# Value product of a top-k attention: the last 64 rows of both heads as one block diagonal matrix that opens the accumulation

## The chip, the cores and the metric

One NeuronCore of one Trainium2 chip. The metric is device time in microseconds (us) of one execution. PE (TensorE) has two queues in the profile: PE for matrix products and PEld for weight loads. DVE is VectorE, ACT is ScalarE, POOL is GpSimd, and SP issues nearly all input transfers. Each engine works through its own instructions in the order in which the program was written, and waits at the first one whose operands are not there.

## The reference

Attention over 2 batches, 8 heads, 576 positions and 64 columns a head, in float32. Of each row of scores only the 32 largest are kept. Its output feeds a first mixture of four experts and a second layer of three products under a maximum.

```python
scores = scale * q @ k.T                                   # 576 x 576 for a batch and head
kth = np.partition(scores, -32, axis=-1)[..., -32:-31]
attn = softmax(np.where(scores >= kth, scores, -1e9))
x = (attn @ v) as [1152, 512]                              # heads side by side
out = sum_e p[:, e:e+1] * (relu(x @ w1[e]) @ w2[e])        # p: domain_probs over their row sum
return max(out @ m1, out @ m2, out @ m3) @ mo
```

## The kernel before

**Pairs.** The attention works on two heads at once, the head pair `hp` (four of them), and on a tile of 128 rows of the 1152 (nine). That gives 36 pairs, in the order chunk `c` (tiles 0 and 1, 2 and 3, 4 and 5, 6 to 8), head pair, tile. A `Pair` goes through: scores on PE (L350), copies of them to SBUF on ACT (L358), four rounds of the eight largest on DVE (L371, L373), the exponential on ACT (L384), and the mask that keeps the 32 largest (`mask`). The mask is one DVE instruction with the row sum (L391), except in the first eight pairs, where `ON_POOL` puts it on POOL as two instructions a head (L394, L395) and the sum on ACT (L399). Then the probabilities are transposed on PE (L409, L414) and copied to SBUF by ACT as `pt[0]`, `pt[1]` (L412) and `pt[2]` (L417). The row sums go through `guard` (ACT, L422), `recip` (DVE, L428), `spread` (ACT, L432) and a transposition (PE, L437), and `norm` (DVE, L462) multiplies the value product by them.

**The value product** (`pv`, L452 and L455). 576 positions are four blocks of 128 and a rest of 64. `pt[0]` and `pt[1]` hold the four blocks of either head; `pt[2]` holds the rest of head 0 in partitions 0 to 63 and that of head 1 in 64 to 127. The tile `vt` of a batch and head pair holds the values in the same way: 4 blocks of 64 columns a head, and a ninth block with the rest of head 0 above that of head 1. Head 0 goes to output partitions 0 to 63, head 1 to 64 to 127. So there are eight products of 128 rows by 64 columns, and after them two of 64 by 64. The tile in the middle (`MIXED`, tile 4) belongs to both batches and is done in two parts of 64 columns each; so 36 pairs make 40 parts.

**Slots.** `attention` writes the order of all engines by slots, eight to a pair: a function is put at a slot, and the slots are then issued one after the other. Pair n begins at slot 8n. `split_k` and `split_q` (ACT L261 and L293, then POOL L262 and L294) and the loads `load_k` and `load_q` (SP, L247) stand some slots before the first pair that needs them. `kraw` and `qraw` have one buffer each, so that a load waits until POOL has split the one before. `load_v` (SP, L266) stands at the slot where the first pair of a batch and head pair begins: pairs 0, 2, 4 and 6 for batch 0, and pairs 16, 18, 20 and 22 for batch 1. The tile `vt` has five buffers. `load_gates` stands at slot 20: a transfer issued by SP (L121), and four small DVE instructions (L123 to L127) that wait for it.

**Products beside it.** From about the eighth pair on, the experts' products (PE, L589 to L591) are woven in between by a count of DVE and PE time. Their weights come through SP (L175) into three buffers, ACT rounds them (`whi`, L224), and POOL (L230, or DVE for some of the late ones) computes the remainder `wlo`. After the last pair only such products are left.

Of the kernel before, what the change touches and what calls it, by code (L numbers as in the profile page):

```python
# [10 lines left out]
F32 = mybir.dt.float32  # L11
# [37 lines left out]
def kernel(  # L49
# [14 lines left out]
    nc = tc.nc  # L64
    B, HP, D, _, S = k.shape
    NT, DM = out.shape
    E = gates.shape[2]
    P = 128
# [3 lines left out]
    NR = S // P  # L72
# [15 lines left out]
    kv = ctx.enter_context(tc.tile_pool(name="kv", bufs=2))  # L88
# [22 lines left out]
    def pe(n):  # L111
        clock["pe"] += n / 2400.0

    def bank(name):
        return pg.tile([P, 512], F32, tag="g", name=name)
# [126 lines left out]
    kraw, kT, vt, qraw, qT = {}, {}, {}, {}, {}  # L242
# [19 lines left out]
            sub(out=d[D:, j], in0=t[D:, j], in1=d[D:, j].bitcast(F32), op=ALU.subtract)  # L262

    def load_v(b, hp):
        t = vt[b, hp] = kv.tile([P, 2 * NR + 1, D], F32, tag="v", bufs=5, name="vt")
        nc.sync.dma_start(out=t, in_=v[b, hp])  # L266

    def load_q(c, hp, heads=slice(0, 2)):
        slots = SLOTS[c]
# [61 lines left out]
    class Pair:  # L331
# [109 lines left out]
        def pv(self):  # L441
            assert {("pt", i) for i in range(3)} <= self.did
            ps = bank("psv")
            pe((NR + 1) * 512)
            if self.t == MIXED:
                parts = [(0, slice(0, TAIL)), (1, slice(TAIL, P))]
            else:
                parts = [(0 if self.t < MIXED else 1, slice(0, P))]
            for b, cols in parts:
                for r in range(NR):  # L450
                    for j in range(2):
                        nc.tensor.matmul(ps[j * D:(j + 1) * D, cols], lhsT=vt[b, self.hp][:, j * NR + r, :],  # L452
                                         rhs=self.pt[j][:, r, cols], start=r == 0, stop=False)
                for j in range(2):
                    nc.tensor.matmul(ps[j * D:(j + 1) * D, cols], lhsT=vt[b, self.hp][j * D:(j + 1) * D, 2 * NR, :],  # L455
                                     rhs=self.pt[2][j * D:(j + 1) * D, cols], start=False, stop=True)
            self.x = ps

        def norm(self):
# [17 lines left out]
    def attention():  # L477
# [18 lines left out]
        for key, n in first_use.items():  # L496
            s0 = 8 * n
            if n == 0:
                if key[0] == "k":
                    at_slot(-60, load_first)  # L500
                    at_slot(-50, split_first)
                    free["k"] = free["q"] = -50
                    at_slot(s0, load_v, *key[1:])
                continue
            load, split = (load_k, split_k) if key[0] == "k" else (load_q, split_q)
            at = max(s0 + options(n)["scores"] - (SPLIT_K if key[0] == "k" else SPLIT_Q), free[key[0]] + 2)
            at_slot(max(at - 15, free[key[0]] + 1), load, *key[1:])
            at_slot(at, split, *key[1:])
            free[key[0]] = at
            if key[0] == "k":  # L510
                at_slot(s0, load_v, *key[1:])
# [129 lines left out]
    def experts(n, c):  # L641
        tiles = CHUNKS[c]
        N = len(tiles) * P
        if c < len(CHUNKS) - 1:
            acc = [xp.tile([P, DM], F32, tag="acc", bufs=sum(len(x) for x in CHUNKS[:-1]), name="acc") for _ in tiles]
        else:

            acc = [kv.tile([P, (2 * NR + 1) * D], F32, tag="v", bufs=5, name="acc")[:, 0:DM] for _ in tiles]
        accs.update(zip(tiles, acc))

        def half1(i, u):
# [262 lines left out]
```

## Time and profile before

| | us |
|---|---|
| Median of three runs | 791.98 |
| Lowest and highest run | 791.22, 792.48 |
| Profiled execution, first to last instruction (its own time) | 793.7 |
| PE busy in it | 737.3 (93%) |
| DVE busy | 659.2 (83%) |
| POOL busy | 533.4 (67%) |
| ACT busy | 480.5 (61%) |

The profiled execution was 1.7 us longer than the median. The attention ends at about 484 us of it; all pairs lie before that and the rest is products. Busy shares are means over stages that differ: in the first 100 us PE is far from full and DVE is not, and after 600 us it is the other way round. A busy PE is not a PE at its peak, since the ends of matrix products are modelled; how fast it works is seen from the starts of its instructions.

### The profile page before, as it was taken

How to read it: one execution, taken by the hardware profiler on the slowest of the kernel's cores; microseconds unless marked ns; L12 is line 12 of the kernel's file. 1: busy time of each engine (PE TensorE's matmuls, PEld its weight loads, DVE VectorE, ACT ScalarE, POOL GpSimd, SP SyncE). 2: the span in 40 equal slices, each digit the busy share in tenths (PEclk: the TensorE clock that was granted, in tenths of full speed). 3: DMA queues.
4: the chain of work that ended last, by engine and by line, in shares of the span. 5: the costliest groups of instructions: out<-in, count | busy, mean ns of one | idle time of the engine just before them, and what ended most of it. 6: DMA issues, size and time to landing. Idle time of an engine off the chain costs nothing.

```text
span 793.7 us, 13648 instructions
## 1 busy us (share of the span) xinstructions
PE 737.3 (93%) x4726; PEld 656.9 (83%) x4726; DVE 659.2 (83%) x1247; ACT 480.5 (61%) x1021; POOL 533.4 (67%) x438
## 2 busy tenths in 40 slices
PE   3776799979999999999999999989999899999998
PEld 2554699879888888988898897978999699899996
DVE  6999989978999999999999996989999783243241
ACT  5666758666776777767777665655565352443441
POOL 2787968859888979688888696667564553253330
PEclk9976699989999999999999999999999999999999
DMA  3430145445466445353644455867878554262421
GB/s 99 119 108 3 52 146 160 139 134 181 116 177 202 126 139 171 116 159 114 168 132 133 134 164 167 293 221 244 263 235 256 168 190 136 93 212 65 169 100 40
DMA packets 48485, 119.92 MB, mean 151 GB/s; under 512 B 7712, under 2 KB 17952, under 8 KB 48416
## 3 DMA queue, kind: packets, MB, share of 16 engines
q1 hardware_dynamic: 40208, 110.40, 45.1%
q10 hardware_dynamic: 8208, 8.65, 3.1%
q8 instruction: 37, 0.61, 0.3%
q14 instruction: 32, 0.26, 0.1%
HBM read 110.38 MB, written 8.65 MB: 150 GB/s over the span
## 4 chain that ended last, share of the span: by engine, by line
PE 43%; DVE 32%; DMA 8%; POOL 6%; issue 5%; ACT 3%; SPq 2%; ACTq 0%; POOLq 0%; DVEq 0%
DVE m L371 12%; PE ps L589 12%; PE ps L591 11%; PE ps L590 11%; DVE work L373 11%; DVE p L391 5%; POOL wlo L230 5%; DMA raw<-in_w_dram 3%; SPq L247 2%; PE pso L591 2%; PE pso L589 2%; PE pso L590 2%; DMA raw<-in_m_dram 2%; DMA kraw<-in_k_dram 2%; ACT whi L224 1%
## 5 line engine op out<-in xcount | busy, mean ns | idle before, releaser
L230 POOL TENSOR_TENSOR wlo<-raw,whi 128x512 fp32r<-128x512 f32 x260 | 354.6, 1391 | 155.7 <-ACT whi L224 154.9
L224 ACT ACTIVATE whi<-raw 128x1024 fp32r<-128x1024 f32 x164 | 170.6, 1058 | 66.9 <-PE ps L591 30.8
L589 PE MATMUL ps<-xl,whi 128*128 128x256 f32 (+1 forms) x512 | 155.0, 303 | 0.8 <-DVE h L669 0.8
L371 DVE MAX8 m<-work 128x8 f32<-128x576 f32 x216 | 154.5, 742 | 0.1
L591 PE MATMUL ps<-xh,wlo 128*128 128x256 f32 (+1 forms) x512 | 152.5, 298 | 0.0
L590 PE MATMUL ps<-xh,whi 128*128 128x256 f32 (+1 forms) x512 | 152.5, 298 | 0.0
L373 DVE MATCH_REPLACE8 work<-m,work 128x576 f32<-128x576 f32 x144 | 106.3, 739 | 0.0
L230 DVE TENSOR_TENSOR wlo<-raw,whi 128x1024 fp32r<-128x1024 f32 x34 | 49.6, 1460 | 66.2 <-ACT whi L224 54.9
L589 PEld LDWEIGHTS ps<-xl,whi 128*128 128x128 f32 x512 | 98.6, 193 | 1.9 <-DVE h L669 1.0
L590 PEld LDWEIGHTS ps<-xh,whi 128*128 128x128 f32 x512 | 98.6, 193 | 0.9
L591 PEld LDWEIGHTS ps<-xh,wlo 128*128 128x128 f32 x512 | 98.6, 193 | 0.0
L589 PE MATMUL ps<-wlo,h 128*128 128x512 f32 x192 | 78.1, 407 | 0.0
L590 PE MATMUL ps<-whi,h 128*128 128x512 f32 x192 | 75.7, 394 | 0.0
L591 PE MATMUL ps<-whi,h 128*128 128x512 f32 x192 | 75.7, 394 | 0.0
L591 PE MATMUL ps<-x2h,wlo 128*128 128x384 f32 x216 | 72.8, 337 | 0.0
L589 PE MATMUL ps<-x2l,whi 128*128 128x384 f32 x216 | 72.8, 337 | 0.0
L590 PE MATMUL ps<-x2h,whi 128*128 128x384 f32 x216 | 72.6, 336 | 0.0
L409 PE MATMUL psp<-ident,p 128*128 128x128 f32 x288 | 49.5, 300 | 24.9 <-POOL p L395 16.4
L391 DVE SCALAR_TENSOR_TENSOR p<-s,m,p 128x576 f32<-128x576 f32 x57 | 72.0, 1263 | 0.0
L350 PE MATMUL pss<-kT,ql 128*128 128x288 f32 x160 | 54.5, 355 | 14.0 <-DVE ql L294 7.5
L207 POOL TENSOR_TENSOR narrow<-narrow,raw 128x256 int32<-128x256 int32 x48 | 38.7, 806 | 42.0 <-DVE narrow L204 11.7
L409 PEld LDWEIGHTS psp<-ident,p 128*128 128x128 f32 x288 | 37.3, 153 | 30.9 <-POOL p L395 19.7
(96 smaller groups left out, 1639.7 us busy)
## 6 DMA issues: line engine op xcount, KB each, us to landing
raw<-in_w_dram SPq DMA_DIRECT2D x128, 512.0 KB, 3.8
raw<-narrow SPq DMA_DIRECT2D x36, 512.0 KB, 3.3
raw<-in_m_dram SPq DMA_DIRECT2D x36, 256.0 KB, 4.6
narrow<-narrow ACTq DMA_DIRECT2D x48, 128.0 KB, 3.8
kraw<-in_k_dram SPq DMA_DIRECT2D x14, 288.0 KB, 4.4
raw<-in_mo_dram SPq DMA_DIRECT2D x12, 256.0 KB, 4.1
vt<-in_v_dram SPq DMA_DIRECT2D x8, 288.0 KB, 4.4
out_dram<-ob ACTq DMA_DIRECT2D x9, 256.0 KB, 2.0
```

The source lines that it names most:

```text
L207: nc.gpsimd.tensor_tensor(out=out.bitcast(I32), in0=out.bitcast(I32), in1=last, op=ALU.add)
L224: nc.scalar.activation(out=hi, in_=raw, func=AF.Copy)
L230: on.tensor_tensor(out=lo[:, x], in0=raw[:, x], in1=hi[:, x].bitcast(F32), op=ALU.subtract)
L247: nc.sync.dma_start(out=out[half * D:(half + 1) * D], in_=src)
L350: nc.tensor.matmul(ps[:, 0:SH], lhsT=l, rhs=r, start=i == 0, stop=i == len(mm) - 1)
L371: nc.vector.max(m[:, 8 * r:8 * r + 8], src)
L373: nc.vector.match_replace(out=self.w[j], in_to_replace=m[:, 8 * r:8 * r + 8], in_values=src, imm_value=NEG)
L391: nc.vector.scalar_tensor_tensor(out=p, in0=s, scalar=kth, in1=p, op0=ALU.is_ge, op1=ALU.mult, accum_out=total)
L409: nc.tensor.transpose(ps[:, r * P:(r + 1) * P], self.p[:, part, part * TAIL + r * P:part * TAIL + (r + 1) * P], ident)
L589: nc.tensor.matmul(ps, lhsT=lh, rhs=rl, start=first, stop=False)
L590: nc.tensor.matmul(ps, lhsT=lh, rhs=rh, start=False, stop=False)
L591: nc.tensor.matmul(ps, lhsT=ll, rhs=rh, start=False, stop=last)
```

## The change

`vt` gets a tenth block of 64 columns. The ninth keeps the rest of head 0 in partitions 0 to 63 and gets zeros in 64 to 127; the tenth gets zeros in 0 to 63 and the rest of head 1 in 64 to 127. Blocks nine and ten side by side are then a block diagonal matrix of 128 by 128. The transfer is the same as before and fills blocks one to nine; three POOL instructions behind it, in `load_v`, clear the upper half of block ten, copy the lower half of block nine into it, and clear that lower half. In `pv` one product of 128 by 128 with `pt[2]` opens the accumulation for both heads, and the eight products of 128 by 64 follow, of which the last ones close it.

```diff
     def load_v(b, hp):
-        t = vt[b, hp] = kv.tile([P, 2 * NR + 1, D], F32, tag="v", bufs=5, name="vt")
-        nc.sync.dma_start(out=t, in_=v[b, hp])
+        t = vt[b, hp] = kv.tile([P, 2 * NR + 2, D], F32, tag="v", bufs=5, name="vt")
+        nc.sync.dma_start(out=t[:, 0:2 * NR + 1], in_=v[b, hp])
+        nc.gpsimd.memset(t[0:D, 2 * NR + 1], 0.0)
+        nc.gpsimd.tensor_copy(out=t[D:, 2 * NR + 1], in_=t[D:, 2 * NR])
+        nc.gpsimd.memset(t[D:, 2 * NR], 0.0)
...
             for b, cols in parts:
+                both = vt[b, self.hp][:, 2 * NR:2 * NR + 2, :].rearrange("p a d -> p (a d)")
+                nc.tensor.matmul(ps[:, cols], lhsT=both, rhs=self.pt[2][:, cols], start=True, stop=False)
                 for r in range(NR):
                     for j in range(2):
                         nc.tensor.matmul(ps[j * D:(j + 1) * D, cols], lhsT=vt[b, self.hp][:, j * NR + r, :],
-                                         rhs=self.pt[j][:, r, cols], start=r == 0, stop=False)
-                for j in range(2):
-                    nc.tensor.matmul(ps[j * D:(j + 1) * D, cols], lhsT=vt[b, self.hp][j * D:(j + 1) * D, 2 * NR, :],
-                                     rhs=self.pt[2][j * D:(j + 1) * D, cols], start=False, stop=True)
+                                         rhs=self.pt[j][:, r, cols], start=False, stop=r == NR - 1)
```

A tile that shares the buffers of `vt` in the last chunk of the experts is made as wide as the new `vt`. Line numbers behind L269 are three higher in the changed kernel until `pv`. The orders of DVE, ACT and SP stay the same; POOL gets 24 instructions, PE loses one product in each of 40 parts.

On POOL, around the first `load_v` (slot 0), before. `ql` and `kT` are the splits of queries and keys, `s` and `p` the mask of pair 0; what a row waits for stands in brackets:

```order
L294 TENSOR_TENSOR ql<-qraw,qh 128x2x256 [waits DMAHW1_49,DMAHW0_49,Activation_49]
L262 TENSOR_TENSOR kT<-kraw,kT 64x576 [waits DMAHW3_49,Activation_49,Pool_49]
L262 TENSOR_TENSOR kT<-kraw,kT 64x576 [waits Activation_49]
L394 TENSOR_SCALAR s<-s,m_188 128x576 [waits DVE_49,Activation_49,Pool_49]
L395 TENSOR_TENSOR p<-p,s 128x576 [waits Pool_49]
L394 TENSOR_SCALAR s<-s,m_196 128x576 [waits DVE_49,Activation_49]
L395 TENSOR_TENSOR p<-p,s 128x576 [waits Pool_49]
L294 TENSOR_TENSOR ql<-qraw,qh 128x2x256 [waits DMAHW4_49,DMAHW5_49,PE_49,Activation_49]
L262 TENSOR_TENSOR kT<-kraw,kT 64x576 [waits DMAHW7_49,Activation_49,Pool_49]
```

The same place on POOL in the changed kernel:

```order
L262 TENSOR_TENSOR kT<-kraw,kT 64x576 [waits Activation_49]
L267 MEMSET vt 64x64
L268 COPY vt<-vt 64x64 [waits DMAHW0_49]
L269 MEMSET vt 64x64 [waits Pool_49]
L397 TENSOR_SCALAR s<-s,m_188 128x576 [waits DVE_49,Activation_49,Pool_49]
L398 TENSOR_TENSOR p<-p,s 128x576 [waits Pool_49]
L397 TENSOR_SCALAR s<-s,m_199 128x576 [waits DVE_49,Activation_49]
L398 TENSOR_TENSOR p<-p,s 128x576 [waits Pool_49]
L297 TENSOR_TENSOR ql<-qraw,qh 128x2x256 [waits DMAHW4_49,DMAHW5_49,PE_49,Activation_49]
L262 TENSOR_TENSOR kT<-kraw,kT 64x576 [waits DMAHW7_49,Activation_49,Pool_49]
```

The three new instructions stand between the key split and the mask of pair 0, and the copy waits for the transfer of `vt`; the mask and the next splits stand behind it.

On PE, at the first value product, before (`pss` are scores, `psv` the value product):

```order
L350 MATMUL pss<-kT,qh 128x288
L350 MATMUL pss<-kT,ql 128x288 [waits Activation_49]
L350 MATMUL pss<-kT,qh 128x288
L452 MATMUL psv<-pt,vt 64x128 [waits DMAHW0_49,Activation_49]
L452 MATMUL psv<-pt,vt 64x128 [waits Activation_49]
L452 MATMUL psv<-pt,vt 64x128 x6
L455 MATMUL psv<-pt_295,vt 64x128 [waits Activation_49]
```

And in the changed kernel:

```order
L353 MATMUL pss<-kT,qh 128x288
L353 MATMUL pss<-kT,ql 128x288 [waits Activation_49]
L353 MATMUL pss<-kT,qh 128x288
L455 MATMUL psv<-pt_298,vt 128x128 [waits DMAHW0_49,Activation_49]
L458 MATMUL psv<-pt,vt 64x128 x8
```

The product with the rest (`pt_295`, now `pt_298`) has moved from the end of the part to its head, and with it the wait for the last copy of ACT.

## Rows read from the trace of the kernel before

**Rows 1.** Page: shares of the chain that ended last, engines, then lines.

```profile
PE 43%; DVE 32%; DMA 8%; POOL 6%; issue 5%; ACT 3%; SPq 2%; ACTq 0%; POOLq 0%; DVEq 0%
```

**Rows 2.** Windows: stretch; busy us (instructions) of PE, PEld, DVE, ACT, POOL; clock, DMA.

```profile
60.00:100.00 40.00, 27.54 (x159) 21.73 (x158) 39.97 (x90) 28.18 (x79) 34.41 (x27) 0.67 0.11 31
100.00:130.00 30.00, 30.00 (x237) 27.44 (x237) 27.29 (x57) 20.87 (x45) 23.62 (x20) 1.00 0.53 162
130.00:180.00 50.00, 45.90 (x333) 40.53 (x332) 45.72 (x93) 32.42 (x71) 36.49 (x32) 0.93 0.43 134
180.00:230.00 50.00, 49.73 (x346) 43.49 (x345) 47.03 (x98) 34.76 (x78) 45.05 (x39) 1.00 0.54 160
```

**Rows 3.** Waits of DVE from 200 to 480 us: total, times, longest.

```profile
DVE acc L698 <- PE ps L591: 0.6, 1, 0.6
```

**Rows 4.** Chain of waits in order of time, start and us, up to 60 us.

```profile
28.08 1.42 POOL kT L262
...
31.31 4.30 DMA gate<-in_gates_dram
```

**Rows 5.** Timeline of DVE: start, us, instruction, idle before it and what ended that.

```profile
29.22 0.15 DVE L428 RECIPROCAL rr<-rs 128x2 f32<-128x2 f32 x1
...
35.63 0.19 DVE L123 TENSOR_REDUCE gs<-gate 128x9 f32<-128x36 f32 x1 [1.45 <-DMA gate<-in_gates_dram]
...
41.46 0.15 DVE L428 RECIPROCAL rr<-rs 128x2 f32<-128x2 f32 x1
```

**Rows 6.** Timeline of POOL around the first load of values.

```profile
16.12 2.77 POOL L262 TENSOR_TENSOR kT<-kraw,kT 64x576 fp32r<-64x576 f32 x2 [1.19 <-ACT kT L261]
18.99 1.73 POOL L394 TENSOR_SCALAR s<-s,m 128x576 f32<-128x576 f32 x1
```

**Rows 7.** Tile view of `vt`, its first transfer: issue, and issue to landing.

```profile
L266 SPq DMA_DIRECT2D vt<-in_v_dram x1: 585/585/585, 20.1 to 20.1; - x1
...
DMA to landing us min/median/max: 4.5/4.5/4.5
```

**Rows 8.** POOL's groups by shape: count, busy us, mean ns of one.

```profile
L475 POOL TENSOR_TENSOR xl<-xt,xh 128x128 fp32r<-128x128 f32 x36 | 20.5, 571 | 3.5 <-ACT xh L474 3.4
L278 POOL MEMSET qraw<- 128x128 f32 x8 | 1.4, 201 | 0.1
```

**Rows 9.** Timeline of PE around a value product at full clock.

```profile
126.11 0.60 PE L409 MATMUL psp<-ident,p 128*128 128x128 f32 x4
126.55 0.27 PE L414 MATMUL psp<-ident,p 128*128 128x128 f32 x1
...
130.92 1.09 PE L452 MATMUL psv<-pt,vt 128*64 128x128 f32 x16
131.94 0.43 PE L455 MATMUL psv<-pt,vt 64*64 64x128 f32 x4
132.31 0.33 PE L437 MATMUL psr<-ident,rb 128*128 128x128 f32 x1
```

**Rows 10.** Timeline of SP: the fifth and the last issue of `vt`.

```profile
209.09 1.45 SPq L266 DMA_DIRECT2D vt<-in_v_dram  x1
...
287.09 0.33 SPq L266 DMA_DIRECT2D vt<-in_v_dram  x1
```

**Rows 11.** Tile view of `vt`: all eight transfers, issue to landing.

```profile
DMA to landing us min/median/max: 3.1/4.4/5.0
```

**Rows 12.** Timeline of POOL behind these two loads, and its next idle times.

```profile
211.17 1.85 POOL L294 TENSOR_TENSOR ql<-qraw,qh 128x768 fp32r<-128x768 f32 x1
...
223.84 1.30 POOL L662 TENSOR_TENSOR h<-raw,h 128x512 fp32r<-128x512 f32 x1 [1.34 <-ACT h L661]
...
289.73 1.86 POOL L294 TENSOR_TENSOR ql<-qraw,qh 128x768 fp32r<-128x768 f32 x1
294.96 5.57 POOL L230 TENSOR_TENSOR wlo<-raw,whi 128x512 fp32r<-128x512 f32 x4 [3.38 <-ACT whi L224]
```

**Rows 13.** Timeline of ACT: a weight that waits for its transfer.

```profile
225.87 1.06 ACT L224 ACTIVATE whi<-raw 128x1024 fp32r<-128x1024 f32 x1 [1.16 <-DMA raw<-in_w_dram]
```

More of the change, by code (lines that the diff above doesn't have):

```diff
@@ L646, in experts @@
         else:
-            acc = [kv.tile([P, (2 * NR + 1) * D], F32, tag="v", bufs=5, name="acc")[:, 0:DM] for _ in tiles]
+            acc = [kv.tile([P, (2 * NR + 2) * D], F32, tag="v", bufs=5, name="acc")[:, 0:DM] for _ in tiles]
         accs.update(zip(tiles, acc))
```

## The prediction

> **What bounds the kernel now.** I read the shares of the chain of waits first: PE 43%, DVE 32% [rows 1]. So two engines take turns, and the question for each part of the change is whose turn it falls into. The windows and DVE's waits answer that. From 60 to 100 us DVE is busy 39.97 of 40 us and PE 27.54 [rows 2]: DVE is the bound. From 100 to 230 us DVE has holes, 2.71 + 4.28 + 2.97 = 9.96 us of 130 [rows 2]: there PE, POOL and the weights lead. From 200 to 480 us DVE waits once, for 0.6 us [rows 3]: it is the bound again, although PE looks nearly full. Behind about 484 us there are only products. All value products lie before that, mostly where DVE leads. A shorter PE can give back little there, while anything that stops DVE is paid in full.
>
> Then I read the start of the chain in order of time. It runs from a key split on POOL, 28.08 us [rows 4], through SP (the next key load had to wait for that split, and the loads of `vt` and of the gates stand behind it) to the transfer of the gates, issued at 31.31 us and landing 4.30 us later [rows 4]. DVE has idled 1.45 us for it when it goes on at 35.63 us [rows 5]. So here POOL's own order already sets DVE's time, and this is where the change puts three instructions.
>
> **PE: one product for two.** At full clock the 16 records of L452 start at 130.92 us, the four of L455 at 131.94, the next instruction at 132.31 [rows 9]. L455 so costs 132.31 - 131.94 = 0.37 us a part; that goes. The new opening product is two records of 128 by 128. Nearest are the four transposes of that size, 0.44 us from the first to the next instruction [rows 9], 0.11 each, so 0.22 us for two. From below: two records at the pace of L452, 1.02 / 16 each, 0.13 us; from above: no cheaper than what it replaces, 0.37 us. I take 0.22, since the transposes have the same shape, and a gain of 0.15 us a part (0 to 0.24). Of the 40 parts 7 lie before 94 us, where DVE leads; 33 remain, 33 x 0.15 = 5.0 us of PE time. What of it reaches the end is bounded by DVE: from 200 us on at most the 0.6 us that DVE waits [rows 3], and before that half a dozen parts, 6 x 0.15 = 0.9 us, in front of a stage that waits for weights as well. I take 0.5 us, and 0 to 2.1 for the range (11 parts at 0.19). The wait for the last copy of ACT comes first instead of last. It can cost a few tenths of a us where PE now waits for ACT before `pv`; those places are mostly in DVE's stretches, and I count nothing.
>
> The four records of L455 take 0.092 us each, those of L452 0.064 [rows 9]: the small ones are no cheaper. The Trainium skill, TensorEngine Tiling (Array Packing), Key Properties, speaks against this half of the change: tiles of the array work in parallel, so two products of 64 by 64 on different rows and columns need no more time than the one that replaces them; it also says that a change of the tiling mode drains the array, and one such change goes. By the first rule alone the gain on PE would be 0 and the sum 0.5 us higher; by both it is the drain, and the 0.15 us agree with that.
>
> **POOL: the first load, the dear one.** POOL finishes two key splits at 16.12 + 2.77 = 18.89 us and begins the mask of pair 0 at 18.99 [rows 6]. In the changed order the two clearings and the copy stand between, and the copy waits for `vt`. SP issues that transfer only at 20.1 us, because it too stands behind a load that waits for these splits, and it lands 4.5 us later [rows 7], at 24.6. So POOL, which works in order, stands still from about 19.1 to 24.6 us. The copy itself isn't in the trace of before; nearest are a clearing of 128 by 128, 0.20 us, and a two-operand instruction of that size, 0.57 us [rows 8]. With half the columns I take 0.25 us for the copy, 0.15 for a clearing and 0.1 for starts: the mask starts at 24.6 + 0.5 = 25.1 instead of 18.99, **6.1 us late** (5.9 to 6.6). Nothing covers it: behind it on POOL are the mask (four instructions without a gap), the query split and the key splits of rows 4, which all move by 6.1. With the key split SP's queue moves, with that the gate transfer, from 31.31 to 37.4 us, and DVE goes on at 37.4 + 4.3 = 41.7 instead of 35.63 us. DVE will already have waited on the way, at the `recip` of 29.22 us [rows 5], since the row sums of pair 0 come after its mask; that wait lies inside the same 6.1 us. From there to 94 us DVE has no holes into which the loss could go, so the whole program moves by 6.1 us.
>
> **The second load.** SP issues its transfer just ahead of the gates, so at about 30.7 + 6.1 = 36.8 us, and by the median of 4.4 us [rows 11] it lands at 41.2. POOL comes there at about 39: the splits end at 28.08 + 1.42 + 6.1 = 35.6 us [rows 4], and the mask of one head follows, 1.73 us [rows 6] and a second instruction nearly as long. It waits 2.2 us and works 0.5. The next `recip`, at 41.46 us [rows 5], moves to 47.6 by itself; the mask of the other head now ends at about 45, and ACT's work between the two fills most of what is left. I count 0, and up to 1.0 for the range. Loads three and four have landed when POOL comes to them: 0.5 us of work each, in POOL's idle time (34.41 of 40 us busy [rows 2]).
>
> **Loads five to eight.** They lie where DVE leads. The fifth is issued at 209.09 us [rows 10], lands 4.4 us later by the median [rows 11], and POOL comes there at 211.17 [rows 12]: it waits 2.3 us. The last: 287.09 + 4.4 - 289.73 = 1.8 us. Four of these at a mean of 2.05, with 0.5 us of work each, are 10.2 us of POOL. POOL's own idle times come next: 1.34 us before 223.84, 3.38 us before 294.96 [rows 12]. So most is caught up before anyone waits. What may get through is a weight: SP's weight loads wait for POOL to free a buffer, and ACT at 225.87 us already waits 1.16 us for one [rows 13], with the next exponential behind it. Of the fifth load's 2.8 us 1.34 are caught up by then; half of the other 1.5 is my price, 0.7 us, from 0 up to half of the 10.2.
>
> **The sum.** 6.1 - 0.5 + 0 + 0.7 = +6.3 us. The profiled span would go from 793.7 to 800.0 us; against the median of the runs, 791.98, that is **798.3 us**, since nothing in the sum depends on the 1.7 us between them.
>
> **The rivals.** (a) The later waits aren't caught up: every us in which POOL stands still at loads five to eight reaches DVE or PE. Then 791.98 + 6.1 - 0.5 + 10.2 = 807.8 us; for it speaks that SP, ACT and POOL hang on each other by three weight buffers, against it POOL's idle times and DVE's single wait of 0.6 us in the whole stretch. (b) The first loss is taken back between 100 and 230 us, where DVE has 9.96 us of holes: 792 us, no change. It needs a stage that is led by weights which are not delayed themselves. Against: their first loads stand on SP behind a load that waits for POOL, and their remainders on POOL behind the masks, so they are late too. (c) Faster: POOL's wait falls into slack that I don't see and PE leads everywhere; then 33 parts at 0.15 give 791.98 - 5.0 = 787.0 us. It decides from the point at which the gate transfer is not what DVE waits for; the 1.45 us of idle with that name speak against it, and so does DVE's full stretch from 200 on. (d) The opening product costs more than it saves; that is a tenth of a us a part in DVE's shadow, within the range of the forecast.
>
> **Chances.** Forecast 0.72, (a) 0.14, (b) 0.08, (c) 0.06. Slower by over 0.2% (above 793.6 us; about what a measurement of this kernel can tell from no change) is forecast and (a), 0.86; within it (b), 0.08; faster (c), 0.06. The range: below, 791.98 + 5.9 - 2.1 and another us for a shifted clock, which runs in steps before 110 us (0.67 of full from 60 to 100 [rows 2]), 794.8; above, 791.98 + 6.6 + 5.1, rounded up for the second load's part, 804.0, half way into (a).
>
> **What would show it.** Right: in the new trace POOL's first mask begins near 25 us with an idle time that ends by the transfer of `vt`; DVE idles about 5 us at its first `recip` and some 3 at the gates; the gates' work starts near 41.7 us; the start of L452 to the instruction behind the part is shorter by about 0.37 us, with some 0.22 in front; and the last pair ends about 6 us later. Wrong: POOL starts its mask at 19 us (the copy did not wait), or DVE's idle time between 100 and 230 us falls by as much as it gained before, or weight loads after 209 us leave DVE holes of 2 us each.

## The result, and the profile after

The changed kernel takes 798.33 us (median of 8 runs, 795.84 to 802.14), the kernel before 792.2 (8 runs, 790.15 to 794.82): 6.1 us more, as forecast. The ratio of the two is 1.0089, with a 95% interval of 1.0065 to 1.0112, so 5 to 9 us. The profiled execution spans 796.4 us; here every run's time is 1.8 us above its span, so that the profiled execution of before, with a span of 793.7, took 795.5 us and was longer than any of these eight. Differences of time are therefore taken from the medians below, and the profiles are used for where time goes. Single executions of one kernel differ by up to 10.6 us (23 runs of before, further down, lie between 785.13 and 795.77), and their granted clocks don't order them (the correlation of time and clock is -0.09 to -0.17 in the three sets of before).

The page of after, part 4: the chain of waits by engine and by line. It answers to [rows 1].

```profile
DVE 38%; PE 37%; DMA 8%; POOL 8%; issue 4%; ACT 3%; SPq 2%; ACTq 0%; POOLq 0%; DVEq 0%
DVE m L374 14%; DVE work L376 13%; PE ps L592 10%; PE ps L594 10%; PE ps L593 10%; DVE p L394 5%; DMA raw<-in_w_dram 4%; POOL wlo L230 3%; DVE h L672 2%; DMA vt<-in_v_dram 2%; PE pso L594 2%; PE pso L592 2%; PE pso L593 2%; SPq L247 2%; POOL kT L262 1%
```

The transfer of `vt`, which nobody had waited for in before, is now on the chain with 2%. DVE's share has grown from 32 to 38%, PE's has fallen from 43 to 37%.

The timeline of POOL at the first two loads (start, us, instruction; in brackets idle time and what ended it), the place of [rows 6]:

```profile
15.88 2.78 POOL L262 TENSOR_TENSOR kT<-kraw,kT 64x576 fp32r<-64x576 f32 x2 [1.75 <-ACT kT L261]
18.72 0.14 POOL L267 MEMSET vt<- 64x64 f32 x1
24.32 0.24 POOL L268 COPY vt<-vt 64x64 f32<-64x64 f32 x1 [5.46 <-DMA vt<-in_v_dram]
24.62 0.15 POOL L269 MEMSET vt<- 64x64 f32 x1
24.86 1.73 POOL L397 TENSOR_SCALAR s<-s,m 128x576 f32<-128x576 f32 x1
...
41.27 0.24 POOL L268 COPY vt<-vt 64x64 f32<-64x64 f32 x1 [2.51 <-DMA vt<-in_v_dram]
```

POOL stands still for 5.46 us and begins the mask of pair 0 at 24.86 us, where it had begun at 18.99. Behind it the chain can be followed step by step. This is the chain of waits of after in order of time (start, us, what):

```profile
18.72 0.16 POOL vt L267
...
19.87 4.40 DMA vt<-in_v_dram
...
24.86 1.73 POOL s L397
...
29.87 1.42 POOL p L398
...
32.59 2.79 POOL kT L262 x2
35.40 0.48 SPq L247
...
37.20 4.14 DMA gate<-in_gates_dram
...
41.36 0.20 DVE gs L123
```

Mask, key split, the key load on SP, the gates, DVE: the chain of [rows 4], with POOL's wait in front. The gates were issued at 31.31 us and are now at 37.20. DVE shows both places at which it stood; its timeline, beside [rows 5]:

```profile
33.30 0.17 DVE L431 RECIPROCAL rr<-rs 128x2 f32<-128x2 f32 x1 [4.12 <-ACT rs L425]
...
41.36 0.19 DVE L123 TENSOR_REDUCE gs<-gate 128x9 f32<-128x36 f32 x1 [3.08 <-DMA gate<-in_gates_dram]
...
47.56 0.14 DVE L431 RECIPROCAL rr<-rs 128x2 f32<-128x2 f32 x1
```

The last row is the `recip` that stood at 41.46 us: 6.10 us late, and so are the instructions that follow it up to 92 us. The four later loads that POOL waits for are in the list of its waits from 200 to 300 us (who waited for what: us in total, times, longest):

```profile
POOL vt L268 <- DMA vt<-in_v_dram: 6.6, 4, 2.1
```

And PE, beside [rows 9], timeline at full clock:

```profile
122.46 0.40 PE L594 MATMUL ps<-whi,h 128*128 128x512 f32 x1
122.69 0.38 PE L455 MATMUL psv<-pt,vt 128*128 128x128 f32 x2
123.01 1.09 PE L458 MATMUL psv<-pt,vt 128*64 128x128 f32 x16
124.03 0.33 PE L440 MATMUL psr<-ident,rb 128*128 128x128 f32 x1
```

From the last product ahead to the instruction behind the part are 124.03 - 122.46 = 1.57 us. Before they were 132.31 - 130.60 = 1.71 (the product ahead of the part in [rows 9] started at 130.60). So a part became 0.14 us shorter.

### The profile page after: what moved, and what is told of

Read it like the earlier page. It is cut to its first block, busy times and chain, and to the rows that moved or that the text cites. A ratio compares the mean times of both kernels' runs of the same rounds, so it can differ in the third digit from the quotient of the medians.

```text
span 796.4 us, 13528 instructions
## 1 busy us (share of the span) xinstructions
PE 733.0 (92%) x4646; PEld 662.8 (83%) x4646; DVE 657.2 (83%) x1247; ACT 482.0 (61%) x1021; POOL 537.7 (68%) x462
## 4 chain that ended last, share of the span: by engine, by line
DVE 38%; PE 37%; DMA 8%; POOL 8%; issue 4%; ACT 3%; SPq 2%; ACTq 0%; POOLq 0%; DVEq 0%
DVE m L374 14%; DVE work L376 13%; PE ps L592 10%; PE ps L594 10%; PE ps L593 10%; DVE p L394 5%; DMA raw<-in_w_dram 4%; POOL wlo L230 3%; DVE h L672 2%; DMA vt<-in_v_dram 2%; PE pso L594 2%; PE pso L592 2%; PE pso L593 2%; SPq L247 2%; POOL kT L262 1%
## 5 line engine op out<-in xcount | busy, mean ns | idle before, releaser
L394 DVE SCALAR_TENSOR_TENSOR p<-s,m,p 128x576 f32<-128x576 f32 x57 | 68.5, 1202 | 0.0
```

What stands on the lines that cost most here:

```text
L394: nc.vector.scalar_tensor_tensor(out=p, in0=s, scalar=kth, in1=p, op0=ALU.is_ge, op1=ALU.mult, accum_out=total)
```

## The experiments

Theory: POOL, in its order, waits for the first transfer of `vt`, and what stands behind it on POOL makes DVE late. Rival 1: the new product, or its earlier wait for ACT's last copy, is the loss. Rival 2: the waits at loads five to eight are. The first four kernels ran on one chip, beside 29 runs of the kernel before (792.45 us).

**The three POOL instructions moved ten slots behind the load.** PE's part is that of the change. `late_v` says for which loads they move, here for all eight.

```diff
         nc.sync.dma_start(out=t[:, 0:2 * NR + 1], in_=v[b, hp])
+        if not late_v(b, hp):
+            fill_v(b, hp)
+
+    def late_v(b, hp):
+        return True
+
+    def fill_v(b, hp):
+        t = vt[b, hp]
         nc.gpsimd.memset(t[0:D, 2 * NR + 1], 0.0)
         nc.gpsimd.tensor_copy(out=t[D:, 2 * NR + 1], in_=t[D:, 2 * NR])
...
                 at_slot(s0, load_v, *key[1:])
+                if late_v(*key[1:]):
+                    at_slot(s0 + 10, fill_v, *key[1:])
```

> The change, with its three POOL instructions ten slots after the load instead of right behind it; PE's part is untouched. Theory (POOL's wait for the transfer of vt is the loss): no wait of POOL for vt, the mask of pair 0 begins near 19 us and the work on the gates near 35.6 us, as before; the time is that of before less what PE gives back, 791.3 to 792.8 us. Rival 1 (the new product or its earlier wait for ACT's last copy is the loss): the time stays near 798. Rival 2 (the waits at loads five to eight are the loss): near 792 as well, so this run does not tell it from the theory.

Measured: 791.44 us (12 runs), ratio to before 0.9983 (0.9963 to 1.0003). Its POOL timeline:

```profile
16.22 2.79 POOL L262 TENSOR_TENSOR kT<-kraw,kT 64x576 fp32r<-64x576 f32 x2 [2.08 <-ACT kT L261]
19.10 1.73 POOL L405 TENSOR_SCALAR s<-s,m 128x576 f32<-128x576 f32 x1
...
25.66 0.23 POOL L276 COPY vt<-vt 64x64 f32<-64x64 f32 x1
```

The mask begins at 19.10 us and the copy waits for nothing. The loss is gone, with the new product in place: rival 1 falls. The work on the gates began at 36.25 us, 0.6 later than in before, since the 0.7 us of POOL work now stood ahead of the query split; the `recip` behind it stood 0.80 us late, at 42.26 us.

**Only the first load keeps them right behind it.** `late_v` is now:

```diff
     def late_v(b, hp):
-        return True
+        return (b, hp) != (0, 0)
```

> As the run before, but the first load alone keeps its three POOL instructions right behind it; the other seven have them ten slots later. Theory: the whole loss of the early stage is back, DVE is 6.1 us late at 60 us, 797.0 to 798.3 us. Rival 1: near 798. Rival 2: near 792, since no wait at loads five to eight is left. Against the change itself it shows what loads two to eight add: 0.7 us by the prediction.

Measured: 796.87 us (12 runs), ratio 1.0055 (1.0032 to 1.0078). DVE's waits from 8 to 100 us (us in total, times, longest):

```profile
DVE rr L439 <- ACT rs L433: 4.2, 1, 4.2
DVE gs L123 <- DMA gate<-in_gates_dram: 3.1, 1, 3.1
```

These are the two waits of the change, and the time, just under the expected range, is 5.4 us above that of late_fill beside it. DVE agrees; its timeline in late_fill and here:

```profile
42.26 0.14 DVE L439 RECIPROCAL rr<-rs 128x2 f32<-128x2 f32 x1
47.63 0.15 DVE L439 RECIPROCAL rr<-rs 128x2 f32<-128x2 f32 x1
```

The `recip` begins 5.37 us later. One load of eight carries most of the loss: rival 2 falls.

**POOL's instructions alone**, with the value product of before. Against the change, the third one clears the half of block ten that was just copied, since block nine has to stay whole for the old product (the expectation calls it the upper half).

```diff
-        nc.gpsimd.memset(t[D:, 2 * NR], 0.0)
+        nc.gpsimd.memset(t[D:, 2 * NR + 1], 0.0)
```

> The three POOL instructions of the change right behind each load, with the value product of before (eight products, then two of 64 by 64; the third instruction clears the upper half of block ten again, so that block nine stays whole). Theory: 798.4 to 799.2 us, the change without the 0.5 us from PE. Rival 1: near 792, as PE does what it did before. Rival 2: near 798.

Measured: 801.48 us (6 runs), ratio 1.0110 (1.0083 to 1.0137). The loss needs nothing of PE's part. But it is 3 us larger than in the change, where 0.5 was expected. The profile shows one place where PE, after a wait, also ran slower, in its timeline:

```profile
308.90 1.11 PE L412 MATMUL psp<-ident,p 128*128 128x128 f32 x4 [2.32 <-DVE h L672]
```

and in the windows behind it (stretch and length; busy us of PE, PEld, DVE, ACT, POOL; granted clock, DMA share, GB/s):

```profile
309.00:312.00 3.00, 3.00 (x15) 3.00 (x16) 3.00 (x6) 0.91 (x2) 3.00 (x4) 0.50 0.39 85
312.00:320.00 8.00, 8.00 (x46) 6.91 (x46) 6.92 (x16) 5.65 (x13) 4.94 (x5) 1.00 0.69 174
```

After 2.32 us of waiting PE ran 3 us at 1.2 GHz, then at 2.4 again. Whether this is the 3 us between the two kernels was left to a repeat, below.

**The two small products left out** of the kernel before, and nothing in their place.

```diff
-                for j in range(2):
-                    nc.tensor.matmul(ps[j * D:(j + 1) * D, cols], lhsT=vt[b, self.hp][j * D:(j + 1) * D, 2 * NR, :],
-                                     rhs=self.pt[2][j * D:(j + 1) * D, cols], start=False, stop=True)
```

> The kernel before without the two products of 64 by 64 in each part: the last 64 positions are left out of the value product, all else stays. PE has 40 times 0.37 us less to do. Theory (DVE leads in most of the attention): 790.0 to 791.8 us, since 0.6 us of DVE's waiting after 200 us and about one before can be saved. If PE led, 33 x 0.37 = 12 us would go: 780.

Measured: 790.93 us (12 runs), ratio 0.9966 (0.9947 to 0.9985). PE has some 15 us less to do (40 x 0.37), and 1.5 to 2.7 of them, by the medians or the ratio, reach the end. So PE's time in the value product lies mostly in the shadow of other work; that from 200 us on this is DVE's is read from [rows 3]. The run also bounds what any rewriting of these two products can give: by the interval, 1.2 to 4.2 us.

The next four ran together, beside 29 runs of before (792.13 us).

**The gates fetched early**, in the kernel before and in three of the changed ones: the transfer is issued at slot -45, and the DVE work on it stays at slot 20.

```diff
+    def fetch_gates():
+        nc.sync.dma_start(out=gate, in_=gates)
     def load_gates():
-        nc.sync.dma_start(out=gate, in_=gates)
...
+        if s == -45:
+            fetch_gates()
```

> The kernel before, with the transfer of the gates issued at slot -45, ahead of the queue behind the key loads; the four DVE instructions on them stay at slot 20. Theory (the key split, the key load and the gates are a chain that sets DVE's time): DVE's wait of 1.45 us for the gates goes and nothing takes its place, 790.5 to 791.5 us where before is 792.2. Rival (the wait is hidden behind another one): no change.

Measured: 791.42 us (12 runs), ratio 1.0000 (0.9983 to 1.0018). The wait for the gates is gone from DVE's waits, but DVE was only 0.7 us earlier behind it, and the runs can't tell that from nothing. The missing half is in the timeline of DVE: the multiplication of the gates, 0.20 us in before, took longer.

```profile
34.77 1.05 DVE L129 TENSOR_TENSOR gate<-gate,gr 128x36 f32<-128x36 f32 x1
```

**The change with early gates.**

> The change, with the gates issued at slot -45. POOL still waits for vt. Theory: DVE keeps the wait of 4.1 us at its first recip, which is behind the mask of pair 0, and loses the 3.1 us at the gates, so it is some 3.0 us late at 60 us instead of 6.1: about 795.2 us where the change alone is 798.3. Rival (DVE's lateness comes from POOL's wait by another way than the gates): 798.

Measured: 799.11 us (6 runs), ratio 1.0092 (1.0065 to 1.0119): nothing gained over the change. That is the rival's time; the way by which it comes about neither side had named. DVE's timeline:

```profile
33.33 0.17 DVE L433 RECIPROCAL rr<-rs 128x2 f32<-128x2 f32 x1 [4.00 <-ACT rs L427]
...
47.40 0.17 DVE L433 RECIPROCAL rr<-rs 128x2 f32<-128x2 f32 x1 [3.08 <-ACT rs L427]
```

The wait for the gates is gone, and 3.08 us appear at the next `recip`, which now starts at 47.40 us instead of 47.56 in the change. It stands behind the mask of pair 1, and that stands on POOL behind the second load. In the change the second load's wait had been hidden in the wait for the gates; two paths, each about 6 us late, ran side by side.

**Late instructions and early gates together.**

> The change with its three POOL instructions ten slots after each load and the gates issued at slot -45. Theory: neither wait is left in the first 60 us; 791.4 less the 2.1 us that the late fill still showed at the gates, 789.3 us (788.5 to 790.5), the fastest of the three orders.

Measured: 788.22 us (12 runs), ratio 0.9957 (0.9935 to 0.9980). It is faster than both kernels, by about 4 us against before and 10 against the change. Here the multiplication of the gates took 0.20 us again, and DVE was 1.6 us earlier than in before from 38 to 78 us.

**Late POOL instructions with the old product**, to have PE's part alone.

> The three POOL instructions ten slots after each load (the third clears the copied half of block ten, so that block nine stays whole), with the value product of before. Beside the run late_fill it gives PE's part alone where POOL waits for nothing. Theory: 792.0 to 793.0 us, 0.5 to 1.0 above late_fill. If PE's part is worth as much here as between pool_only and the change (3.1 us), it is 794.5.

Measured: 791.73 us (12 runs), ratio 1.0001 (0.9984 to 1.0017), where late_fill had 0.9983. The new product is worth 0.3 to 1.4 us by medians or ratios, which these runs can't tell from nothing.

The last four ran beside 23 runs of before (792.44 us).

**Only the first load's instructions right behind it, gates early.** This tells apart whether the 3.08 us at the second `recip` belong to the second load.

> As after_gates_early, but only the first load keeps its three POOL instructions right behind it; the others have them ten slots later. In after_gates_early DVE was 2.8 us late behind the gates and then lost 3.1 us more at the second recip. Theory: that second loss belongs to the second load, whose wait the gates had covered; here it is gone, DVE stays about 2.8 us late from 37 us on, and the time is 793 to 795 us. Rival (the second loss follows from the first load alone): DVE 6.0 us late at 60 us and 796 to 798 us.

Measured: 793.39 us (12 runs), ratio 1.0020 (0.9994 to 1.0046). DVE's timeline:

```profile
33.58 0.17 DVE L441 RECIPROCAL rr<-rs 128x2 f32<-128x2 f32 x1 [4.28 <-ACT rs L435]
...
44.66 0.14 DVE L441 RECIPROCAL rr<-rs 128x2 f32<-128x2 f32 x1
```

The first wait stays, the second is gone, and the second `recip` starts at 44.66 us, 3.2 late instead of 6. Loads three to eight were moved as well, so the time alone would not tell which load it was; the timeline does, since up to 47 us POOL has come to the first two only (in the change it comes to the third at 59.95 us). So the second loss is the second load's, and it decides DVE's time there as soon as the gates don't.

**Only loads five to eight right behind their transfers.**

```diff
     def late_v(b, hp):
-        return True
+        return b == 0
```

> The change with the POOL instructions of loads one to four ten slots late and those of loads five to eight right behind their loads. It measures what the waits of 209 to 290 us cost by themselves. Prediction: 0.7 us over late_fill (791.4), so 792.1; by the difference between the change and first_only it would be 1.5 us, 792.9. Rival (a) of the prediction, all of these waits reach the end: 801.

Measured: 792.45 us (12 runs), ratio 0.9998 (0.9978 to 1.0018). Against late_fill these waits cost 1.0 us by the medians, 1.2 by the ratios. POOL's waits from 200 to 310 us show them in full:

```profile
POOL wlo L230 <- ACT whi L224: 8.6, 7, 2.6
POOL vt L276 <- DMA vt<-in_v_dram: 6.0, 4, 2.4
```

In late_fill POOL's waiting for weights in the same stretch was longer:

```profile
POOL wlo L230 <- ACT whi L224: 12.3, 7, 3.4
```

So beside 6.0 us of waiting for `vt` and some 2 of work POOL waited 3.7 us less for weights. Not all the rest is hidden from DVE. The windows from 200 to 310 us (stretch and length; busy us of PE, PEld, DVE, ACT, POOL; clock, DMA share, GB/s) of late_fill, of this run and of the change:

```profile
200.00:310.00 110.00, 106.71 (x829) 96.37 (x828) 109.59 (x229) 82.29 (x178) 95.65 (x90) 1.00 0.53 156
200.00:310.00 110.00, 103.86 (x798) 93.67 (x797) 107.56 (x222) 77.44 (x170) 92.59 (x87) 0.98 0.52 154
200.00:310.00 110.00, 106.58 (x833) 96.85 (x832) 105.44 (x227) 81.88 (x178) 98.71 (x91) 1.00 0.52 158
```

DVE has 0.41, 2.44 and 4.56 us of holes there. From 310 to 480 us it is the other way round, with 2.82, 1.28 and 0 us. In all, DVE idles only 0.5 us more here than in late_fill; why the holes set each other off was not tried. Rival (a) of the prediction falls by the time, which is 8.5 us under the 801 that it asks for.

**The change and its POOL part once more**, side by side.

> The change once more, beside the next run: 797.5 to 799.0 us.

> The POOL instructions of the change with the value product of before, once more. Between this run and the one before lies PE's part where POOL waits. If the 3.1 us seen at first were a lower clock behind a wait of PE in a few executions, the difference here is 0.5 to 1.5 us; if PE's part is really worth more once POOL is late, it is again about 3 us.

Measured: 799.35 us (6 runs), ratio 1.0085 (1.0054 to 1.0115), and 800.96 us (6 runs), ratio 1.0102 (1.0071 to 1.0133). The difference is 1.6 us, just above the 0.5 to 1.5 expected for a lower clock in a few executions, and the intervals overlap. The place in the timeline of PE is there again in the second profile:

```profile
308.38 0.66 PE L412 MATMUL psp<-ident,p 128*128 128x128 f32 x4 [1.96 <-DVE h L672]
```

Behind it the granted clock was 0.50 from 309.7 to 313 us. In the profiles of the change and of its repeat PE waited 1.1 and 0.8 us at this place, and the clock stayed at 1.00 from 300 to 320 us. So the lower clock is in both profiles with the old product and in neither with the new one. Behind it DVE waits 1.1 and 1.2 us for a product, which it does not in the change; the lower clock can be that part of the difference. How much PE's part is worth where POOL is late stays open between 0 and 3 us.

## Why the prediction was right, point by point

**What bounds the kernel.** Confirmed: without the two small products, some 15 us of PE, the kernel gains 1.5 to 2.7 us.

**PE, -0.5 us.** The opening product takes 123.01 - 122.69 = 0.32 us to the start of the next, of which some 0.09 are the entry into the products of 64 columns that was paid before, too (130.92 - 130.60 - 0.23, the pace of the products ahead). That leaves 0.23; the prediction had 0.22, and 0.15 gained a part where 0.14 were measured. This holds for the parts of 128 columns. The prediction took it for all 33 parts; in the four pairs done in two parts of 64 columns nothing was gained, 1.96 us from the product ahead to the instruction behind in before (231.90 to 233.86 us) and 1.98 in the change (237.49 to 239.47). Rival (d) falls with these numbers, as (c) does with the result. The earlier wait for ACT's last copy, counted as nothing, is in late_fill too. At the end late_fill is 1.0 us below before, which its 12 runs can't tell from nothing; the term of 0.5 is neither confirmed nor refuted.

**The first load, +6.1 us.** DVE was 6.10 us late. The single numbers held as well: the copy took 0.24 us (0.25), a clearing 0.15, the mask started at 24.86 us (25.1), DVE waited 4.12 us at the `recip` (about 5) and 3.08 at the gates (some 3), and went on at 41.36 us (41.7). In time, first_only lies 5.4 us above late_fill; late_fill was itself 0.8 us late in DVE, and the two differ by 5.37 there. DVE's lateness and the time agree.

**The second load, 0.** The term was right, its reason was not complete. I had the next `recip` moved by the first loss and "just fits" behind it. It fits, but only because the gates make DVE as late: take them away, and the same load costs 3.1 us at that `recip`. It was a second path of the same length, not a hidden wait with room.

**Loads five to eight, +0.7 us.** POOL waited 6.6 us there in the change, where the terms of the prediction give 8.2; at the end it was 1.0 us, by later_only against late_fill. The size was right; the reason, that POOL's own waiting for weights covers most, only in part. That waiting fell from 12.3 us in late_fill to 8.6 in later_only, but DVE also had holes from 200 to 310 us that late_fill had not, 2.0 us more in later_only and 4.2 in the change. Holes of 2 us each behind 209 us were the prediction's sign of being wrong; the longest in the change is 1.5 us. They did not reach the end in full, since DVE idled less behind 310 us.

**The sum.** By the runs -1.0 + 5.4 + 1.0 = 5.4 us; measured 6.1 by the medians, 7 by the ratio. (The -1.0 is late_fill against before; it holds PE's part and the 0.8 us by which that kernel is late itself.) The rest, with loads two to four in it, is below what the runs resolve. That the point itself was met is in part luck: medians of the same kernel differed by 1 us from one set of runs to another (798.33 and 799.35).

**One step was wrong without effect on the sum:** the profiled execution of before was not 1.7 us over the median in its own time but some 3, since a run's time is 1.8 us more than its span. The sum goes from the median and does not use it; the span came to 796.4 us, not to the 800.0 of the prediction. But the readings of before are readings of a long execution, and two of them suffer by it.

One is the sign that the last pair ends about 6 us later. The last `norm` on DVE, in before, in the change and in late_fill:

```profile
483.40 0.29 DVE L462 TENSOR_TENSOR xt<-psv,r 128x128 f32<-128x128 f32 x1 [3.15 <-ACT r L439]
487.82 0.29 DVE L465 TENSOR_TENSOR xt<-psv,r 128x128 f32<-128x128 f32 x1 [4.71 <-ACT r L442]
480.90 0.29 DVE L473 TENSOR_TENSOR xt<-psv,r 128x128 f32<-128x128 f32 x1 [3.38 <-ACT r L450]
```

It is 4.42 us later than in before and 6.92 later than in late_fill. The two comparisons differ by 2.5 us, so a pair of single profiles does not settle a term of this size over so long a stretch.

The other is **rival (b)**, that the stretch from 100 to 230 us takes the loss back. DVE's holes there fell from 9.96 us to 130 - 122.30 = 7.7. But in late_fill, where there is no such loss to take back, they are 130 - 123.62 = 6.4 us. The windows of the change and of late_fill:

```profile
100.00:230.00 130.00, 124.52 (x892) 113.39 (x892) 122.30 (x257) 90.38 (x196) 107.48 (x92) 0.95 0.49 145
100.00:230.00 130.00, 126.17 (x920) 114.36 (x918) 123.62 (x255) 90.87 (x197) 108.54 (x95) 0.97 0.54 159
```

So the fall shows nothing of the rival's kind, and it is far from the 6.1 that the rival needed.

## What to carry to other kernels

A preparation that waits for a transfer belongs on an in-order engine at the point where its data have landed, not at the point where the transfer is issued: moved by ten slots, the same three instructions cost nothing that could be measured in the time (791.44 us where before had 792.45), though DVE stood 0.8 us later behind the gates. Before a few tenths of a us are saved on one engine, see what waits behind each new instruction on the engine that has to do the preparation, and whether the saving lies where that engine leads at all. And where two paths are late by the same amount, removing one shows nothing; the test that counts removes both, or each without the other.

## What the runs showed of the hardware beside that

Two products of 64 by 64 on different quarters of the array took 0.37 us from their start to the instruction behind them, one full product of 128 by 128 took 0.23. The starts of the single records at full clock show where this comes from. At a steady pace both are alike: two records of the full product are 0.11 us apart, and so are two pairs of small records. But at each change of the form of the products, from 128 by 128 to 128 by 64, from there to 64 by 64, or back, the next record starts 0.09 to 0.10 us later than at that pace: 0.20 us after the one before it from 131.74 to 131.94 us in before, where L455 begins, and 0.21 from 122.80 to 123.01 in the change. Where the new form comes in pairs, the second pair is 0.05 us late as well. Before, a part has three such changes, in the change two; the one that goes, with its late second pair, makes the 0.14 us. The Trainium skill, TensorEngine Tiling (Array Packing), Key Properties, says that a change of the tiling mode drains the array; the trace agrees in so far as each change of form has its price, and does not show what it is made of. This also answers the prediction's question: by the rule of parallel tiles alone nothing would have been gained, and by the pace alone nothing is; the gain is the switch.

The multiplication of the gates on DVE, 128 by 36 elements, took 0.20 us in before, 0.56 in the change and 1.05 in gates_early, with the same operands. The timelines of the change and of late_fill_gates_early, POOL and DVE:

```profile
41.81 1.72 POOL L397 TENSOR_SCALAR s<-s,m 128x576 f32<-128x576 f32 x1
42.05 0.56 DVE L127 TENSOR_TENSOR gate<-gate,gr 128x36 f32<-128x36 f32 x1
...
33.53 1.72 POOL L407 TENSOR_SCALAR s<-s,m 128x576 f32<-128x576 f32 x1
34.69 0.20 DVE L129 TENSOR_TENSOR gate<-gate,gr 128x36 f32<-128x36 f32 x1
```

In the seven profiles in which no POOL instruction ran beside it, it took 0.20 us. In five (the change, its repeat, pool_only, its repeat and first_only_gates_early) it began 0.22 to 0.33 us behind a mask instruction of POOL with one large operand, and ended 0.78 to 0.79 us behind that one's start, whenever it had begun; in late_fill_gates_early it began 1.17 us behind such a start and took 0.20. In gates_early it ended 0.05 us behind the end of a POOL instruction on two large operands (34.37 us plus 1.40). So its length goes with what POOL has just begun. What stretches it was not tried by itself.
